# A decayed attention kernel with a feed-forward layer behind it: a second small fetch at the start, and fillers in other places

## The chip, the cores and the metric

The kernel runs on one core of a Trainium2 chip. The metric is the time of one execution on the device, in microseconds (us), as the median of several runs. Of the kernel before, three runs are shown: 191.89, 191.92 and 194.59 us. The core has five engines with instruction streams of their own: TensorE (PE, matmul and its weight loads), VectorE (DVE), ScalarE (ACT), GpSimd (POOL) and SyncE (SP, which here only issues transfers). Sixteen DMA engines move data between the chip's memory (HBM) and the on-chip memory (SBUF). Matmuls write to PSUM.

## The reference

The first half is causal attention with a decay: each of 8 heads has a number lam near 1, and the score of query i and key j counts with lam to the power of i - j. It is computed in blocks of 64 positions, with a state that is carried from block to block.

```python
B, H, S, D = 4, 8, 768, 64
for b in range(S // 64):
    intra = (qb @ kb.T) * Dmask          # Dmask[i, j] = lam ** (i - j) for i >= j, else 0
    out_b = intra @ vb + (qb * lam ** (pos + 1)) @ kv_state
    kv_state = lam ** 64 * kv_state + (kb * lam ** (63 - pos)).T @ vb
```

The second half takes the attention's output as 3072 tokens of 512 numbers through a layer of 2048 hidden numbers:

```python
h = x @ w_in
g = h * sigmoid(1.702 * h)
out = g @ w_out
```

All inputs and the output are float32; q, k and v have the shape [4, 8, 768, 64].

## The kernel before, in words

The sequence is cut into six row tiles of 128 positions (the program's w = 0 to 5), and in each tile all 4 batch entries and all 8 heads are done. The first two tiles (w = 0 and 1) are laid out in another way than the rest: each is done in two halves of the batch (c = 0 and 1), with 256 positions of two batch entries in one tile of 128 partitions. For every tile the kernel loads k, q and v, multiplies k and q by powers of lam while it casts them to bfloat16 (`do_cast`, line 202 or 210), turns them so that the head dimension lies on the partitions, multiplies k by q to scores, masks them (line 271), and multiplies them by v. For w = 0 and 1 the turning is done by TensorE against an identity matrix (`turn_pe`, the matmuls at line 239), and the result is copied out of PSUM by ScalarE (line 222) or VectorE (line 219). For the later tiles a transposing transfer does it (line 246). The feed-forward layer of one tile runs while the next tile's attention is made ready.

What matters here are the first ten microseconds, up to the masks of the first half tile. The order of events in the program is this:

1. ScalarE issues the fetch of `lam_r`, 8 numbers in one partition (line 105). SP issues the loads of k, q and v for w = 0, c = 0, each in two pieces of 256 KB, and then k and q for c = 1 (line 84). ScalarE loads the table for exponentials and logarithms.
2. TensorE runs "fillers": matmuls of a tile of zeros with itself, 512 columns wide, whose result nobody reads (`fill`, line 147). Behind four of them stands the matmul that spreads lam over all 128 partitions (line 151).
3. ScalarE takes the logarithm of lam (line 153) and makes the powers for the casts from it by exponentials (lines 156, 658 and 661), then loads the table for the later activation function (line 663).
4. VectorE casts k in two groups of heads, TensorE turns both, and the same follows for q. Between the turns stand fillers: two behind k's first turn, one behind k's second, one behind q's first, none behind q's second.
5. GpSimd waits at `gate_pool` (line 651) until the second piece of q is there, and only then issues the first load of `w_in` and v for c = 1.
6. The scores (line 260) and the masks on VectorE (line 271) follow.

The order of the work is set in two ways. The part up to the powers (steps 1 to 3) is ordered by the framework's scheduler, which places each instruction on its engine when, by its own reckoning, its inputs are ready. Everything inside `with tc.manual_schedule()` is written out by hand and keeps its order within itself; the scheduler may still take an instruction of that part ahead of one of the first part on the same engine. Each engine then works through its list in order. A transfer carries one of eight semaphores for its completion, handed out in turn, and a new transfer waits until the last one with the same semaphore is done.

SBUF is laid out by pools. The tiles of the pool `const` stand behind one another in the order in which they are made, and the other pools (`ld` for the loads, `work` for casts and turned tiles, `op` for outputs and partial sums) follow behind them.

Of the kernel before, what the change touches and what calls it, by code (L numbers as in the profile page):

```python
# [25 lines left out]
def kernel(  # L26
# [13 lines left out]
    nc = tc.nc  # L40
    f32 = mybir.dt.float32
    bf16 = mybir.dt.bfloat16
    B, H, S, D = q.shape
    P = 128
# [20 lines left out]
    const = ctx.enter_context(tc.tile_pool(name="const", bufs=1))  # L65
# [37 lines left out]

    lam_r = const.tile([1, H], f32)
    nc.scalar.dma_start(out=lam_r, in_=bass.AP(tensor=lam.tensor, offset=lam.offset, ap=[[0, 1], [1, H]]))
    ones = const.tile([1, P], f32)
    nc.vector.memset(ones, 1.0)
    load(0)
# [31 lines left out]
    def acc(name, dt=f32, shape=None, tag="a"):  # L140
        return ps.tile(shape or [P, 4, P], dt, tag=tag, bufs={"a": 5, "mm": 3}[tag], name=name)

    def fill(n, new=None):
        if new:
            fill_ps[0] = acc("ps_fill", shape=[P, W], tag=new)
        for _ in range(n):
            nc.tensor.matmul(fill_ps[0], zero[:, 0:P], zero, start=True, stop=True)  # L147

    fill(4, "mm")
    lam_p = ps.tile([P, H], f32, tag="a", bufs=5, name="lam_p")  # L150
    nc.tensor.matmul(lam_p, ones, lam_r, start=True, stop=True)
    ln_lam = const.tile([P, H], f32)
# [40 lines left out]
    def do_cast(w, c, nm, eng, g=None):  # L193
        if g in (None, 0):
            cast[w, c, nm] = work.tile([P, NP, 2, P] if w < ND else [P, 2, HD], bf16, tag=f"{nm}s{c}",
                                       bufs={"k": 2, "q": 1}[nm], name=f"{nm}s")
        f, x = loaded[w, c, nm], cast[w, c, nm]
        if w < ND:
            pw = {"k": kd_pow, "q": qd_pow}[nm]
            for R in (0, 1) if g is None else (g,):  # L200
                h = slice(4 * R, 4 * R + 4)
                eng.tensor_tensor(x[:, 2 * R : 2 * R + 2].rearrange("p i a (j d) -> p j (i a) d", j=2),
                                  f[:, h].rearrange("p (j i) (a d) -> p j (i a) d", j=2, a=2),
                                  pw[:, h].rearrange("p (j i) a -> p j (i a)", j=2).unsqueeze(3).to_broadcast([P, 2, 4, D]),
                                  op=MUL)
        else:
            pw = {"k": k_pow, "q": q_pow}[nm]
            n = 2 * H // 4
            for j in range(2):
                eng.tensor_tensor(x.rearrange("p b (r i j d) -> p j (b r) i d", i=2, j=2, d=D)[:, j],  # L210
                                  f.rearrange("p h (a d) -> p (h a) d", a=2).rearrange("p (n j i) d -> p j n i d", j=2, i=2)[:, j],
                                  pw.rearrange("p b (r j i) -> p j (b r) i", i=2, j=2)[:, j].unsqueeze(3).to_broadcast([P, n, 2, D]),
                                  op=MUL)
# [19 lines left out]
    def turn_pe(w, c, nm, copy=act_copy, g=None):  # L233
        x = cast[w, c, nm]
        rr = list(range(NP)) if g is None else [2 * g, 2 * g + 1]
        t = acc("ps_t", bf16, [P, len(rr), 2, P])
        for i, r in enumerate(rr):
            for a in range(2):
                nc.tensor.transpose(t[:, i, a, :], x[:, r, a, :], ident)  # L239
        if g in (None, 0):  # L240
            trans[w, c, nm] = work.tile([P, 2 * NP, P], bf16, tag=f"{nm}T{c}", bufs={"k": 1, "q": 2}[nm], name=f"{nm}T")
        copy(trans[w, c, nm][:, 2 * rr[0] : 2 * rr[0] + 2 * len(rr)], t.rearrange("p r a s -> p (r a) s"))
# [407 lines left out]
    def gate_pool(x):  # L650
        nc.gpsimd.tensor_copy(behind_q, x)  # L651
# [4 lines left out]
    with tc.manual_schedule():  # L656
# [4 lines left out]
            nc.scalar.activation(blk_pow[rows].rearrange("p (r i) -> p r i", i=2),  # L661
                                 ln_lam[rows].rearrange("p (r j i) -> p r j i", i=2, j=2)[:, :, j, :], EXP, scale=1.0 * P)
        nc.scalar.activation(warm, q_pow[:, 0, 0:1], GELU)
        fill(3)
        for nm, copies in (("k", (dve_copy, act_copy)), ("q", (act_copy, dve_copy))):
            for g in range(2):
                do_cast(0, 0, nm, nc.vector, g)
            for g in range(2):
                turn_pe(0, 0, nm, copies[g], g)
                fill(2 - g if nm == "k" else 1 - g)  # L670
        gate_pool(loaded[0, 0, "q"][0:1, H // 2, 0:1])
        load_w_in(0)
        load_one(0, 1, "v", v)
# [99 lines left out]
        for i, (c, fc) in enumerate(halves):  # L773
# [8 lines left out]
            if i in (1, 2, 3, 4):  # L782
                nm = "kq"[(i - 1) % 2]
# [37 lines left out]
```

## Time and profile before

| | |
|---|---|
| median of three runs | 191.92 us (191.89 to 194.59) |
| the profiled execution | 192.3 us |
| its span, first to last instruction | 190.6 us |
| TensorE busy | 184.3 us, 97% |
| VectorE busy | 152.0 us, 80% |
| ScalarE busy | 129.8 us, 68% |
| GpSimd busy | 50.7 us, 27% |
| moved by DMA | 33.91 MB, 178 GB/s on average |

The profile is one execution, recorded by the hardware. Its page gives the busy time of each engine, and the chain that ended last: followed back from the last instruction, at each step to what released it. Beside the page the trace can be asked for the timeline of one engine (start, length, line, operation, tiles, and in brackets the idle time before with what ended it), for the transfers in a stretch of time (queue, packets, MB, share of the 16 engines' time) and for the time from issue to landing. "PEld" are TensorE's weight loads, "SPq" and "ACTq" the issuing instructions of SP and ScalarE.

### The profile page before, as it was taken

What the parts mean: (1) busy time and instruction counts of PE and PEld (TensorE: products, weight loads), DVE (VectorE), ACT (ScalarE), POOL (GpSimd) and SP (SyncE); (2) the same over time, 40 slices, a digit from 0 to 9 for tenths busy, and PEclk for the clock granted to TensorE, in tenths of its full rate; (3) what the DMA queues carried; (4) which work ended last, traced back from release to release, by engine and by line L of the source; (5) the groups of instructions that cost most, each with busy time, mean ns of one, the idle gap of its engine ahead of it and who ended that gap; (6) DMA issues with size and microseconds to landing.
All of it is one profiled execution on the core that took longest, in us unless ns stands there. A gap on an engine that the chain in (4) does not pass through costs nothing.

```text
span 190.6 us, 5527 instructions
## 1 busy us (share of the span) xinstructions
PE 184.3 (97%) x2296; PEld 152.2 (80%) x2296; DVE 152.0 (80%) x282; ACT 129.8 (68%) x242; POOL 50.7 (27%) x69
## 2 busy tenths in 40 slices
PE   7998999999999999999999999999999999999993
PEld 2556646887888888888888888888888888888882
DVE  1787599987856799879799879799789797888950
ACT  4957665169776986388895388885488876597611
POOL 5588000063458000294000393000492000000000
PEclk9999999999999999999999999999999999999999
DMA  5999999996997899988998565999555903300113
GB/s 144 317 292 204 205 206 224 310 302 158 215 276 165 193 221 237 215 192 143 213 236 204 183 164 118 212 242 217 184 142 123 209 1 111 112 5 0 55 56 112
DMA packets 89599, 33.91 MB, mean 178 GB/s; under 512 B 67430, under 2 KB 89446, under 8 KB 89574
## 3 DMA queue, kind: packets, MB, share of 16 engines
q1 hardware_dynamic: 84676, 28.84, 60.5%
q0 software_dynamic: 4896, 4.72, 14.4%
q8 instruction: 18, 0.29, 0.7%
q14 instruction: 7, 0.06, 0.1%
q10 hardware_dynamic: 2, 0.00, 0.0%
HBM read 27.26 MB, written 6.29 MB: 176 GB/s over the span
## 4 chain that ended last, share of the span: by engine, by line
PE 92%; DVE 4%; ACT 2%; issue 0%; ACTq 0%; DVEq 0%
PE ps_X L468 22%; PE ps_hX L559 17%; PE ps_V L468 10%; PE ps_hV L559 8%; PE ps_Q L468 6%; PE ps_h L406 5%; PE ps_h L418 5%; PE ps_hQ L559 4%; DVE sm L271 3%; PE ps_t L239 2%; PE ps_s L339 2%; PE ps_o L394 2%; PE ps_fill L147 2%; PE ps_o L381 1%; PE ps_Z L468 1%; PE ps_s L260 1%
## 5 line engine op out<-in xcount | busy, mean ns | idle before, releaser
L468 PEld LDWEIGHTS <-g_s 128*128 128x128 bf16 x384 | 37.0, 98 | 4.9
L578 ACT ACTIVATE g_sb<-h_sb 128x512 bf16<-128x512 f32 x54 | 32.6, 631 | 1.2 <-DVE h_sb L567 1.2
L559 PEld LDWEIGHTS <-w_in_t 128*128 128x128 bf16 x288 | 28.1, 98 | 3.3
L468 PEld LDWEIGHTS <-g_sb 128*128 128x128 bf16 x288 | 27.5, 98 | 4.1
L222 ACT COPY part<-ps_hX 128x512 f32<-128x512 f32 x32 | 18.3, 587 | 11.5 <-PE ps_hX L559 11.5
L468 PE MATMUL ps_X<-w_out_t,g_s 128*128 128x256 bf16 x192 | 23.3, 273 | 0.0
L559 PEld LDWEIGHTS <-w_in 128*128 128x128 bf16 x216 | 21.1, 98 | 2.5
L559 PE MATMUL ps_hX<-x_s,w_in_t 128*128 128x256 bf16 x144 | 21.6, 272 | 0.0
L445 DVE TENSOR_TENSOR g_s<-g_sb 128x1024 bf16<-128x1024 bf16 x24 | 16.3, 687 | 5.8 <-ACT g_sb L578 5.6
L210 POOL TENSOR_TENSOR ks<-kf,k_pow 128x512 bf16<-128x512 f32 x16 | 16.3, 1042 | 4.8 <-DMA kf<-in_k_dram 4.8
L210 POOL TENSOR_TENSOR qs<-qf,q_pow 128x512 bf16<-128x512 f32 x16 | 16.5, 1056 | 3.1 <-DMA qf<-in_q_dram 3.1
L219 DVE COPY part<-ps_hV 128x512 f32<-128x512 f32 x18 | 12.4, 688 | 5.9 <-PE ps_hV L559 5.9
L651 POOL CAST behind_q<-x_s 1x1 f32<-1x1 bf16 x3 | 0.5, 176 | 58.5 <-DVE x_s L544 58.5
L484 ACT COPY part<-ps_X 128x512 f32<-128x512 f32 (+1 forms) x13 | 6.7, 518 | 13.2 <-PE ps_X L468 13.2
L567 DVE TENSOR_TENSOR h_sb<-part,ps_hX 128x512 f32<-128x512 f32 x18 | 12.3, 681 | 2.6 <-PE ps_hX L559 2.1
L567 DVE TENSOR_TENSOR h_sb<-part,ps_hV 128x512 f32<-128x512 f32 x18 | 12.3, 684 | 1.0 <-PE ps_hV L559 1.0
L468 PE MATMUL ps_X<-w_out,g_sb 128*128 128x256 bf16 x96 | 12.6, 273 | 0.0
L468 PE MATMUL ps_Q<-w_out,g_sb 128*128 128x256 bf16 x96 | 12.5, 273 | 0.0
L567 DVE TENSOR_TENSOR h_sb<-part,ps_hQ 128x512 f32<-128x512 f32 x18 | 12.2, 680 | 0.0
L222 ACT CAST v_sb<-vf 128x1024 bf16<-128x1024 f32 (+1 forms) x14 | 12.0, 869 | 0.0
L578 ACT ACTIVATE g_sb<-ps_hX 128x512 bf16<-128x512 f32 x18 | 10.6, 589 | 1.8 <-PE ps_hX L559 1.8
L468 PE MATMUL ps_V<-w_out_t,g_s 128*128 128x256 bf16 x96 | 11.6, 273 | 0.0
(113 smaller groups left out, 354.3 us busy)
## 6 DMA issues: line engine op xcount, KB each, us to landing
kf<-in_k_dram SPq DMA_DIRECT2D x10, 512.0 KB, 6.4
qf<-in_q_dram SPq DMA_DIRECT2D x10, 512.0 KB, 7.2
vf<-in_v_dram SPq DMA_DIRECT2D x10, 512.0 KB, 6.2
out_dram<-o_sb SPq DMA_DIRECT2D x24, 128.0 KB, 2.4
out_dram<-o_sb SPq DMA_DIRECT2D x12, 256.0 KB, 2.8
w_out<-in_moe_w_out_dram POOLq DMA_DIRECT2D x4, 512.0 KB, 14.2
kf<-in_k_dram SPq DMA_DIRECT2D x4, 256.0 KB, 3.1
qf<-in_q_dram SPq DMA_DIRECT2D x4, 256.0 KB, 4.6
```

Of the source, the lines that this page charges most:

```text
L210: eng.tensor_tensor(x.rearrange("p b (r i j d) -> p j (b r) i d", i=2, j=2, d=D)[:, j], f.rearrange("p h (a d) -> p (h a) d", a=2).rearran ...
L219: nc.vector.tensor_copy(out, in_)
L222: nc.scalar.copy(out, in_)
L271: nc.vector.tensor_tensor(sm.rearrange("p i a s -> p i (a s)"), flat, mask_d.rearrange("p o a b s -> p o (a b s)").to_broadcast([P, 2, 2 * ...
L406: nc.tensor.matmul(h, w_in_sb[j][:, kc, i * P : (i + 1) * P], xT[w][:, kc, :], start=(kc == 0), stop=(kc == KC - 1))
L418: nc.tensor.matmul(h[:, u, :], w_in_sb[j][:, kc, i * P : (i + 1) * P], xT[w][:, kc, cols], start=(kc == 0), stop=(kc == KC - 1))
L445: nc.vector.tensor_tensor(o, x, y, op=f)
L468: nc.tensor.matmul(bank[:, t], x[:, m, t * P : (t + 1) * P], y, start=((n in (1, 2, 7) or own) and t == ts[0] * last and m == 0), stop=(m ...
L484: nc.scalar.copy(part[w, n, t.start][:, t], bank[:, t])
L559: nc.tensor.matmul(bank[:, u], z[:, kc], y[:, kc], start=(n in (1, 2, 7) and u + kc == 0), stop=(kc == 1), skip_group_check=True)
L567: nc.vector.tensor_tensor(h, h_part[w, g, {2: 1, 5: 7, 4: 6}[n]], bank, op=ADD)
L578: nc.scalar.activation(g_of[w][:, a : b + 1 : b - a, 256 * i : 256 * i + 256], bank, GELU)
```

## The change

It has three parts. A new tile `first_q`, one number in each of 128 partitions, is fetched behind lam on ScalarE's queue. It takes one number of q for every 3072 (12 KB), over the first quarter of q, which is the first batch entry. Nothing reads the tile. Then the program asks for two fillers ahead of lam's matmul in place of four, and for four in place of three at the start of the hand-ordered part. Last, the fillers between the turns: one behind k's first and two behind k's second (before: two and one), and none behind q's (before: one behind the first).

```diff
     nc.scalar.dma_start(out=lam_r, in_=bass.AP(tensor=lam.tensor, offset=lam.offset, ap=[[0, 1], [1, H]]))
+    first_q = const.tile([P, 1], f32)
+    nc.scalar.dma_start(out=first_q, in_=bass.AP(tensor=q.tensor, offset=q.offset, ap=[[H * S * D // P, P], [1, 1]]))
     ones = const.tile([1, P], f32)
...
-    fill(4, "mm")
+    fill(2, "mm")
     lam_p = ps.tile([P, H], f32, tag="a", bufs=5, name="lam_p")
     nc.tensor.matmul(lam_p, ones, lam_r, start=True, stop=True)
...
-        fill(3)
+        fill(4)
         for nm, copies in (("k", (dve_copy, act_copy)), ("q", (act_copy, dve_copy))):
             for g in range(2):
                 do_cast(0, 0, nm, nc.vector, g)
             for g in range(2):
                 turn_pe(0, 0, nm, copies[g], g)
-                fill(2 - g if nm == "k" else 1 - g)
+                fill(1 + g if nm == "k" else 0)
```

## The prediction

> **What bounds the kernel now.** I read the page first, for the share of each engine; then the chain that ended last over the first 20 us, because every edit lies there; then the timeline of single engines beside it; and last the transfers of the later stages, for what a slower or faster stream would reach.
>
> The page's busy times and its chain:
>
> ```profile
> span 190.6 us, 5527 instructions
> PE 184.3 (97%) x2296; PEld 152.2 (80%) x2296; DVE 152.0 (80%) x282; ACT 129.8 (68%) x242; POOL 50.7 (27%) x69
> PE 92%; DVE 4%; ACT 2%; issue 0%; ACTq 0%; DVEq 0%
> ```
>
> TensorE is the bound: of 190.6 us it is idle for 6.3. A change that leaves the stream of matmuls alone can only win or lose at the edges. This is the edge at the start, as the chain's pieces from 1.39 us on (start, length, work):
>
> ```profile
> 1.39 1.89 PE ps_fill L147 x4
> 3.28 0.54 PE lam_p L151 x2
> ...
> 4.64 0.70 DVE ks L202
> ...
> 5.39 0.61 PE ps_t L239 x4
> 6.00 0.85 PE ps_fill L147 x2
> 6.85 0.43 PE ps_t L239 x4
> 7.28 0.43 PE ps_fill L147
> 7.71 0.44 PE ps_t L239 x4
> ...
> 8.17 0.59 ACT qT L222
> ...
> 8.80 0.47 PE ps_s L260 x16
> ...
> 9.33 2.48 DVE sm L271 x4
> ```
>
> The reader is to see that the start is a single file: four fillers, lam's matmul, its logarithm and powers on ScalarE, the cast of k, then on TensorE k's two turns and q's first turn with three fillers among them, the copy of q, the scores, the masks. From 9.33 VectorE's masks set the pace. So a filler ahead of q's first turn costs its full 0.43 us, and one behind it costs nothing until it touches the masks.
>
> **The change part by part.**
>
> *lam's matmul.* Is it the fillers that hold it, or lam's transfer? The queue of ScalarE's transfers, asked for 1.5 to 1.8 us:
>
> ```profile
> q10 hardware_dynamic: 2, 0.00, 0.3%
> ```
>
> Both packets of lam move in that stretch, so lam is there well before 3.28 and the fillers hold its matmul. Two fillers fewer would be worth having. But the words of the change are not what the built program holds. There the order on TensorE is decided by the framework's scheduler, which pulls fillers out of the hand-ordered part to fill the time that it reckons for lam's transfer. In the changed program four fillers stand ahead of lam's matmul, as before; two follow where three did. So lam's matmul, the powers and k's cast stay where they are: 0 us.
>
> *The fillers behind lam.* The stretch up to k's first turn, on TensorE:
>
> ```profile
> 3.73 1.46 PE L147 MATMUL ps_fill<-zero 128*128 128x512 bf16 x3
> 5.38 0.35 PEld L239 LDWEIGHTS <-ks 128*128 128x128 bf16 x4 [1.10 <-DVE ks L202]
> ```
>
> k's first turn waits for the cast that ends at 5.34, while the third filler's columns end near 5.0. One filler less leaves the turn at 5.39: 0 us. From there the counts are 1, 2, 0 in place of 2, 1, 1 (behind k's first turn, k's second, q's first). Up to q's first turn that is three fillers either way: a turn's matmuls follow each other for 0.43 (the 0.61 of the first has a tail of 0.18 in it), so k's second turn starts at 5.39 + 0.43 + 0.43 = 6.25 (its cast, the second of a pair of 0.70 each from 4.64, is ready by 6.04), the two fillers at 6.68, q's first turn at 7.53, and it is out at 7.53 + 0.61 = 8.14, against 7.71 + 0.44 = 8.15 now. Sum 0. k's second turn is out 0.43 us sooner and q's second about as much, and both meet a closed door:
>
> ```profile
> 7.32 0.59 ACT L222 COPY kT<-ps_t 128x512 bf16<-128x512 bf16 x1
> 6.38 1.28 DVE L202 TENSOR_TENSOR qs<-qf,qd_pow 128x512 bf16<-128x512 f32 x2
> 8.62 0.42 DVE L219 COPY qT<-ps_t 128x512 bf16<-128x512 bf16 x1 [0.96 <-PE ps_t L239]
> ```
>
> ScalarE copies k's second turn at 7.32, when it is through with its own powers and its second table load, and with all of that the change has nothing to do. q's second copy moves from 8.62 to about 8.3, but the masks behind it on VectorE wait for scores that need q's first copy, which stays at 8.17 to 8.76. The masks start at 9.33 as before: 0 us.
>
> *The unread piece of q.* Its issue stands on ScalarE between lam's and the table load:
>
> ```profile
> 0.81 0.51 ACTq L105 DMA_DIRECT2D lam_r<-in_lam_dram  x1
> 1.34 1.28 ACT L110 ACT_TABLE_LOAD   x1 [1.34 <-PEq L805]
> 3.84 0.18 ACT L153 ACTIVATE ln_lam<-lam_p 128x8 f32<-128x8 f32 x1 [1.21 <-PE lam_p L151]
> ```
>
> The row of lam's own issue gives 0.51 us. The table load then ends at 3.13 instead of 2.62, and the logarithm waits until 3.84: hidden, with 0.7 us to spare (if lam were early, this would be the next thing late). Its 128 packets of 4 bytes, 8 on each of the 16 engines, join the stream of k and q. A stretch of 1 us of that stream, first 6 to 7 us, then 4 to 5 us:
>
> ```profile
> q1 hardware_dynamic: 664, 0.33, 109.6%
> q1 hardware_dynamic: 387, 0.19, 79.0%
> ```
>
> A packet takes 1.096 x 16 / 664 = 26 ns in the one and 33 ns in the other, so 8 of them delay the stream by 0.21 to 0.26 us if a tiny packet costs as much as one of 512 bytes, and by nearly nothing if it costs by its bytes; I take 0.2. k is taken up at 4.64, and q's second half here:
>
> ```profile
> 6.98 0.72 POOL L651 COPY behind_q<-qf 1x1 f32<-1x1 f32 x1 [3.59 <-DMA qf<-in_q_dram]
> 5.92 1.86 SPq L84 DMA_DIRECT2D qf<-in_q_dram  x2
> ```
>
> GpSimd waits for q's second half until 6.98 and then issues w_in and v. With 0.2 us of delay the second half's cast ends at 6.38 + 1.28 + 0.2 = 7.86, and q's second turn, which stands at 7.53 + 0.43 = 7.96 now that no filler is before it, is still on time: 0 on the path. The new transfer also takes a place in the round of eight completion semaphores, so that SP's issue of q for the second half of the batch, at 5.92, waits for it instead of for k's first transfer. Issued at about 1.3, ahead of q's own, it lands before q's second half, which is there at 6.98: between nothing and 1 us on a transfer that is first read behind the masks, at 9.33 + 2.48 = 11.81. I take nothing.
>
> *Addresses.* The new tile takes 32 bytes, and in the built program every tile made after it moves by 32. The loads' targets (kf, qf, vf), the stores' source (o_sb) and both sides of the transposing transfers stood at multiples of 256 bytes and now stand 32 beyond one. No row of this case has such a transfer, so I bound it: from nothing to twice as long. What it meets first is the third row tile's q, at the end of which the cover is thinnest:
>
> ```profile
> 47.60 5.01 SPq L88 DMA_DIRECT2D qf<-in_q_dram  x2
> 54.70 2.28 POOL L210 TENSOR_TENSOR qs<-qf,q_pow 128x512 bf16<-128x512 f32 x2 [3.07 <-DMA qf<-in_q_dram]
> 61.66 1.26 SPq L246 DMA_TRANSPOSE qT<-qs  x1
> qT<-qs SPq DMA_TRANSPOSE x2, 2.7
> 65.18 0.62 PE L339 MATMUL ps_s<-qT,kT 64*128 64x128 bf16 x16
> ```
>
> From issue to use q takes 54.70 - 47.60 = 7.1 us, from there GpSimd runs without a gap, and the last transpose lands at 61.66 + 2.7 = 64.36, 0.82 us before the scores. A lengthening up to 0.82 / 7.1 = 12% is hidden. I take the end near nothing, because the nearest rows show the stream not at a fixed rate per packet (26 and 33 ns above), so it is not the write of a packet that sets the pace.
>
> [...]
>
> Sum: 0 on the chain, at most 0.1 from the stream. The profiled execution took 192.3 us (span 190.6); the median of the three runs shown is 191.92, 0.4 lower. Against that median I forecast **192.0 us**.
>
> **The rivals.**
>
> *1. The change does what it says.* lam's matmul starts two fillers, 0.85 us, sooner. The logarithm could then start when the table load ends, 3.13 in place of 3.84: 0.7 us off the whole chain, 191.2. For it: lam is there. Against it: the order in the built program, which the trace of before follows to the instruction. Chance 0.04.
>
> *2. The piece of q opens q's memory ahead of time.* The stretch of 4 to 5 us, where q's transfers begin, moves 387 packets against 664 later. If that is a first touch and the new packets take it over, q lands up to (664 - 387) / 664 = 0.42 us sooner, w_in and v with it. On the chain q waits for TensorE, not for its transfer, so between nothing and all of it would pass, at some later edge: 191.6 at best. Chance 0.11.
>
> *3. TensorE's clock comes later.* The same three fillers as at 3.73, after the turns:
>
> ```profile
> 9.45 0.82 PE L147 MATMUL ps_fill<-zero 128*128 128x512 bf16 x3
> 8.20 0.39 PE L239 MATMUL ps_t<-ident,qs 128*128 128x128 bf16 x4
> ```
>
> They take 0.82 in place of 1.46 us, and the turn at 8.20 is already as short: the clock doubles at about 8 us, though the granted clock reads full throughout. The change leaves TensorE idle for 0.6 us before k's first turn in place of 0.2. If the doubling then comes later, the 16 scores ahead of the masks take 0.94 in place of 0.47, and most of the rest lies beside the masks: +0.5, 192.5, and 0 if it comes before 8.8. Chance 0.14. [...]
>
> *4. The shifted addresses slow the transfers: slower than before.* Place: q's load of the third row tile, then v's load of the next ones. Price: what it lengthens beyond the cover. v's row of the fourth row tile:
>
> ```profile
> 89.41 2.78 SPq L88 DMA_DIRECT2D vf<-in_v_dram  x2
> vf<-in_v_dram SPq DMA_DIRECT2D x2, 512.0 KB, 5.7
> 97.08 1.05 ACT L222 CAST v_sb<-vf 128x1024 bf16<-128x1024 f32 x1
> ```
>
> Its cover is 97.08 - 89.41 - 5.7 = 2.0 us. With 25% longer transfers q costs 1.8 - 0.8 = 1.0 and v nothing: 193. With 45%, 2.4 at q and (2.6 - 2.0) x 3 = 1.8 at v: 4.2, 196.2, and there lies the point from which it is slower by over 2%. Twice as long would be 6.3 and (5.7 - 2.0) x 3 = 11.1, 209. For it: the later stages read tiles whose loads have a cover of 1 to 2 us only. Against it: the packets' times above, which vary with what is read. Chance 0.11, half of it beyond 2%.
>
> **How the numbers follow.** Forecast 0.60 at 192.0, rivals 0.04, 0.11, 0.14 and 0.11. A difference under 2% (3.8 us) is about what a measurement of this kernel can't tell from no change; only rival 4 beyond 45% passes it on the slow side, to which I add 0.005 for what I don't see: 0.06. On the fast side nothing passes it, since the whole start before the masks holds less than 1 us of such waits: 0.01. The range goes from rival 1 at 191.2 to 194.2, which takes in the clock, transfers longer by a third at q (2.3 - 0.8 = 1.5, 193.5), and most of the spread of the three runs shown, which reach 194.59 with nothing changed.
>
> **What would show it.** In the profile after: four fillers and lam's matmul at 3.2 to 3.3; the table load at 1.85; k's first turn at 5.39; q's first turn near 7.5 and no filler between it and the second; the masks at 9.3. Rival 1 shows as lam's matmul near 2.4, rival 2 as more than 387 packets from 4 to 5 us, rival 3 as fillers after the scores that still take 1.4 us, rival 4 as scores of the third row tile later than 65.18 behind a transpose. I am wrong if the masks start more than 0.3 us off 9.33, or if TensorE's idle time beyond 20 us grows.

## The result

The kernel after takes **193.5 us** (median of 22 runs, 192.8 to 194.29). The kernel before, run beside it as often, takes 192.74 us (191.89 to 194.82). The ratio of after to before is **1.0032, with a 95% interval of 1.0016 to 1.0048**: the change makes the kernel about 0.3%, or 0.6 us, slower (the two medians by themselves are 0.76 us apart). That is well under the 2% that count as a difference, but more than the runs leave to chance. The profiled execution took 193.21 us, with a span of 191.4 us.

The page of after: its first lines, the largest transfer queue (packets, MB, share of the time of 16 DMA engines), and the shares of the chain that ended last.

```profile
span 191.4 us, 5524 instructions
...
PE 184.9 (97%) x2294; PEld 152.3 (80%) x2294; DVE 151.3 (79%) x282; ACT 130.0 (68%) x242; POOL 50.4 (26%) x69
...
q1 hardware_dynamic: 84676, 28.84, 69.5%
...
PE 74%; DMA 14%; DVE 3%; POOL 3%; SPq 2%; ACT 1%; issue 1%; POOLq 0%; ACTq 0%
```

The same queue on the page of before:

```profile
q1 hardware_dynamic: 84676, 28.84, 60.5%
```

The busy times of the engines are within 1 us of those of before. Two lines have moved. The same 84676 packets with the same bytes now take 69.5% of the DMA engines' time in place of 60.5%: 0.605 x 16 x 190.6 us / 84676 = 21.8 ns a packet before, 0.695 x 16 x 191.4 / 84676 = 25.1 ns after, 15% more. And the chain that ended last, 92% TensorE before, now goes through transfers for 14% of its length.

First the start, as the timeline of TensorE, ScalarE, VectorE and GpSimd in after (start, length, work, idle time before with what ended it):

```profile
1.39 1.89 PE L149 MATMUL ps_fill<-zero 128*128 128x512 bf16 x4 [1.39 <-DVE zero L119]
3.21 0.59 PE L153 MATMUL lam_p<-lam_r,ones 1*128 1x8 f32 x2
3.73 1.03 PE L149 MATMUL ps_fill<-zero 128*128 128x512 bf16 x2
5.38 0.60 PE L241 MATMUL ps_t<-ident,ks 128*128 128x128 bf16 x4 [0.62 <-DVE ks L204]
...
7.49 1.27 PE L241 MATMUL ps_t<-ident,qs 128*128 128x128 bf16 x8
...
1.35 0.40 ACTq L107 DMA_DIRECT2D first_q<-in_q_dram  x1
1.78 1.28 ACT L112 ACT_TABLE_LOAD   x1 [1.78 <-PEq L807]
3.83 0.18 ACT L155 ACTIVATE ln_lam<-lam_p 128x8 f32<-128x8 f32 x1 [0.77 <-PE lam_p L153]
...
7.40 0.69 DVE L204 TENSOR_TENSOR qs<-qf,qd_pow 128x512 bf16<-128x512 f32 x1 [0.20 <-DMA qf<-in_q_dram]
...
9.55 2.48 DVE L273 TENSOR_TENSOR sm<-ps_s,mask_d 128x512 bf16<-128x512 f32 x4 [0.32 <-PE ps_s L262]
...
7.43 0.70 POOL L653 COPY behind_q<-qf 1x1 f32<-1x1 f32 x1 [4.06 <-DMA qf<-in_q_dram]
```

Four fillers still stand ahead of lam's matmul, and two behind it. k's first turn is where it was, the two turns of q follow each other without a filler, and the masks begin at 9.55 in place of 9.33. The second piece of q lands at 7.43 in place of 6.98, and VectorE's second cast of q waits 0.20 us for it.

Next the stretch from 10 to 46 us, where TensorE loses most of the rest. GpSimd, VectorE, SP and TensorE in before:

```profile
22.04 0.43 DVE L535 TENSOR_TENSOR w_in_t<-w_in 128x512 bf16<-128x512 bf16 x1 [1.67 <-DMA w_in<-in_moe_w_in_dram]
...
38.24 1.29 DVE L202 TENSOR_TENSOR qs<-qf,qd_pow 128x512 bf16<-128x512 f32 x2
40.10 0.69 DVE L482 TENSOR_TENSOR part<-part,ps_X 128x512 f32<-128x512 f32 x1 [0.57 <-PE ps_X L468]
...
29.05 0.77 SPq L654 DMA_DIRECT2D behind<-w_out  x1
...
10.50 3.03 POOL L181 DMA_DIRECT2D w_in<-in_moe_w_in_dram  x4
...
40.71 2.05 POOL L202 TENSOR_TENSOR ks<-kf,kd_pow 128x512 bf16<-128x512 f32 x2 [0.71 <-DMA kf<-in_k_dram]
...
39.83 0.61 PE L239 MATMUL ps_t<-ident,qs 128*128 128x128 bf16 x8
...
43.84 0.62 PE L239 MATMUL ps_t<-ident,ks 128*128 128x128 bf16 x8
```

The same instructions in after:

```profile
23.40 0.43 DVE L537 TENSOR_TENSOR w_in_t<-w_in 128x512 bf16<-128x512 bf16 x1 [2.80 <-DMA w_in<-in_moe_w_in_dram]
...
39.44 1.29 DVE L204 TENSOR_TENSOR qs<-qf,qd_pow 128x512 bf16<-128x512 f32 x2
40.64 0.68 DVE L484 TENSOR_TENSOR part<-part,ps_X 128x512 f32<-128x512 f32 x1
...
30.45 0.77 SPq L656 DMA_DIRECT2D behind<-w_out  x1
...
11.18 3.04 POOL L183 DMA_DIRECT2D w_in<-in_moe_w_in_dram  x4
...
42.86 2.04 POOL L204 TENSOR_TENSOR ks<-kf,kd_pow 128x512 bf16<-128x512 f32 x2 [1.19 <-DMA kf<-in_k_dram]
...
40.25 0.93 PE L241 MATMUL ps_t<-ident,qs 128*128 128x128 bf16 x8
...
44.45 0.91 PE L241 MATMUL ps_t<-ident,ks 128*128 128x128 bf16 x8
...
66.09 0.62 PE L341 MATMUL ps_s<-qT,kT 64*128 64x128 bf16 x16
```

The reader is to see two arms that start at one late transfer. VectorE waits 2.80 us for w_in in place of 1.67, and starts on it at 23.40 in place of 22.04, 1.36 us later. Half of that was there when w_in was issued: GpSimd issues four of its loads from 11.18 on in place of 10.50, because they stand behind its wait for q's second piece (0.45 us later) and behind a cast of k that in after waits 0.24 us for k's transfer. The other half came while w_in was on its way. From 23.40 on VectorE has one short gap (0.35 us for the next piece of w_in, 0.36 in before) until its casts of the second row tile's first half are done: q's cast ends at 39.44 + 1.29 = 40.73 in place of 39.53, and where VectorE had 0.57 us to wait for TensorE at 40.10, it now has none. TensorE's turn of q at 40.25 is stretched from 0.61 to 0.93, because its second half waits for that cast. The other arm goes through SP, whose loads for that row tile stand behind VectorE's work on w_out (the row "behind", 29.05 and 30.45, 1.4 us later). v and k for the second half then come late to GpSimd: k's cast starts at 42.86 in place of 40.71, and ends at 44.9 in place of 42.8. Before, TensorE came to that turn at 43.84, 1.1 us behind the cast; now the turn at 44.45 waits for its second half and takes 0.91 in place of 0.62.

So TensorE is late by 0.22 us at the masks, by about 0.6 behind q's turn, by about 0.85 behind k's, and by 0.91 at the third row tile's scores (66.09 against 65.18). From there it loses nothing more: the two spans differ by 0.8 us.

### The profile page after: what moved, and what is told of

Its sections match the earlier page's. It is cut to its first block, busy times and chain, and to the rows that moved or that the text cites. A ratio compares the mean times of both kernels' runs of the same rounds, so it can differ in the third digit from the quotient of the medians.

```text
span 191.4 us, 5524 instructions
## 1 busy us (share of the span) xinstructions
PE 184.9 (97%) x2294; PEld 152.3 (80%) x2294; DVE 151.3 (79%) x282; ACT 130.0 (68%) x242; POOL 50.4 (26%) x69
## 3 DMA queue, kind: packets, MB, share of 16 engines
q1 hardware_dynamic: 84676, 28.84, 69.5%
## 4 chain that ended last, share of the span: by engine, by line
PE 74%; DMA 14%; DVE 3%; POOL 3%; SPq 2%; ACT 1%; issue 1%; POOLq 0%; ACTq 0%
PE ps_X L470 19%; PE ps_hX L561 16%; PE ps_V L470 9%; PE ps_hV L561 8%; DMA w_in<-in_moe_w_in_dram 6%; PE ps_Q L470 5%; DMA vf<-in_v_dram 4%; PE ps_hQ L561 4%; PE ps_h L420 4%; DMA kf<-in_k_dram 3%; PE ps_s L341 2%; PE ps_o L396 2%; SPq L84 2%; POOL ks L204 2%; DVE w_out_t L434 1%; PE ps_o L383 1%
## 6 DMA issues: line engine op xcount, KB each, us to landing
w_out<-in_moe_w_out_dram POOLq DMA_DIRECT2D x4, 512.0 KB, 14.4
```

## The experiments

Three theories could explain it, and the expectations written down ahead of the runs call them by these letters.

- **A, the addresses.** The new tile moves every tile behind it by 32 bytes, off multiples of 256 bytes, and each transfer to or from them gets slower. In a later set, A1 says that the loads' targets (kf, qf, vf) carry most of it, and its rival that the transposing transfers and the stores do.
- **B, the fetch.** The tiny packets of q (ScalarE's queue moves 146 packets in after and 2 in before) delay the stream at the start.
- **C, the clock.** The fillers in other places leave TensorE idle longer before k's first turn (0.62 us in after, 0.20 in before), and its matmuls get faster later. In before three fillers take 1.46 us at 3.73 and 0.82 at 9.45, with the granted clock at 1.00 in both stretches; that this is a clock was the author's reading.

### The shift alone

The kernel before, with a tile that nothing uses:

```diff
     nc.scalar.dma_start(out=lam_r, in_=bass.AP(tensor=lam.tensor, offset=lam.offset, ap=[[0, 1], [1, H]]))
+    pad = const.tile([P, 1], f32)
     ones = const.tile([1, P], f32)
```

> The kernel before with one unused 32-byte tile where the change has its new one: no fetch, the old fillers, and every later tile 32 bytes further, as in the change. Theory A (the shifted addresses lengthen SP's transfers, and the late loads stall the edge near 45 us): SP's queue takes 69 to 70% of the 16 engines' span in place of 60.5%, q's second piece lands 0.3 to 0.5 us later than 6.98, and the time is 1.002 to 1.004 of before. Theory B (the new fetch's own packets delay the first loads): 60 to 61%, ratio 1.000. Theory C (TensorE's clock comes later because fillers are fewer): ratio 1.000, masks at 9.33.

Measured: 1.0071 (1.0045 to 1.0097) of before, from 6 runs where the other experiments have 12. The queue on its page, and the scores of the third row tile on TensorE behind the first four:

```profile
q1 hardware_dynamic: 84676, 28.84, 68.8%
```

```profile
66.91 0.51 PE L340 MATMUL ps_s<-qT,kT 64*128 64x128 bf16 x12 [0.68 <-DMA qT<-qs]
```

Without any fetch and with the old fillers the queue's share rises as in after, and the kernel is slower, by more than theory A expected. Another part of that expectation failed: q's second piece was there at 7.09, 0.1 us later than before and not 0.3 to 0.5, so the cost isn't bound to that one piece. Here one sees as well the wait that the prediction had named for rival 4: the scores of the third row tile stop for 0.68 us, until q's transposing transfer has landed.

### The change without the shift

The change, with its new tile 256 bytes wide in each partition, of which the fetch still fills 4:

```diff
-    first_q = const.tile([P, 1], f32)
-    nc.scalar.dma_start(out=first_q, in_=bass.AP(tensor=q.tensor, offset=q.offset, ap=[[H * S * D // P, P], [1, 1]]))
+    first_q = const.tile([P, 64], f32)
+    nc.scalar.dma_start(out=first_q[:, 0:1], in_=bass.AP(tensor=q.tensor, offset=q.offset, ap=[[H * S * D // P, P], [1, 1]]))
```

> The whole change, but the new tile is 256 bytes wide (one number of it is fetched, as in the change), so the later tiles stand at multiples of 256 bytes again. Theory A: SP's queue back at 60 to 61%, ratio to before 1.000 to 1.001. Theory B: the first loads stay as late as in the change (q's second piece near 7.4), ratio 1.003. Theory C: masks at 9.5, ratio 1.001 to 1.002.

Measured: 1.0009 (0.9985 to 1.0034). The queue and, on VectorE, w_in and the masks:

```profile
q1 hardware_dynamic: 84676, 28.84, 60.8%
```

```profile
9.55 2.48 DVE L273 TENSOR_TENSOR sm<-ps_s,mask_d 128x512 bf16<-128x512 f32 x4 [0.54 <-PE ps_s L262]
...
22.31 0.42 DVE L537 TENSOR_TENSOR w_in_t<-w_in 128x512 bf16<-128x512 bf16 x1 [1.71 <-DMA w_in<-in_moe_w_in_dram]
```

All three edits of the change are in, only the addresses are as before, and share and wait for w_in (1.71 against 1.67) are those of before. The time alone would not settle it, since its interval reaches to 1.0034. But the shift by itself is slower with nothing else in it, and what it brings, the share and the late w_in, is gone here: the addresses make the slowdown. The masks at 9.55 are here too, and cost nothing that the time shows.

### The fillers alone

The kernel before with the change's three edits of `fill`, and no fetch:

```diff
-    fill(4, "mm")
+    fill(2, "mm")
...
-        fill(3)
+        fill(4)
...
-                fill(2 - g if nm == "k" else 1 - g)
+                fill(1 + g if nm == "k" else 0)
```

> The kernel before with only the fillers of the change (2 asked for ahead of lam, 4 behind, then 1, 2, 0, 0), no new fetch and no new tile. Theory C: the fillers after the scores take 1.0 us or more in place of 0.82, the masks start at 9.5 in place of 9.33, ratio 1.001. Theories A and B: masks at 9.33, ratio 1.000.

Measured: 0.9999 (0.998 to 1.0019). GpSimd's wait for q's second piece, the scores on TensorE and the masks on VectorE:

```profile
7.15 0.70 POOL L651 COPY behind_q<-qf 1x1 f32<-1x1 f32 x1 [3.77 <-DMA qf<-in_q_dram]
...
8.80 0.69 PE L260 MATMUL ps_s<-qT,kT 64*64 64x128 bf16 x32 [0.25 <-ACT qT L222]
...
9.33 0.69 DVE L271 TENSOR_TENSOR sm<-ps_s,mask_d 128x512 bf16<-128x512 f32 x1 [0.31 <-PE ps_s L260]
```

The scores of the run before this one, which has the same fillers:

```profile
8.80 1.07 PE L262 MATMUL ps_s<-qT,kT 64*64 64x128 bf16 x32 [0.25 <-ACT qT L224]
```

The fillers cost nothing, and the masks are at 9.33 as before. The 32 scores start at 8.80 in both runs, behind the same instructions, and take 0.69 us here and 1.07 there: the moment at which the matmuls get faster differs between these two profiles, and the 9.55 of after isn't bound to the fillers. C falls. The run before this one has the fetch and this one has not, so whether chance or the fetch moves that moment is open: with the fetch and lam where it was, the 32 scores take 1.00 to 1.12 us in all four profiles; of the seven without it six are fast (0.69 to 0.72, or two halves of 0.42 each), and one (the rest off, below) takes 1.23. Over the kernels here whose lam is where it was, the masks start anywhere from 9.03 to 9.66, with old and new fillers alike.

### The fetch alone

The kernel before with the fetch, in a tile of 256 bytes as above, and the old fillers:

```diff
     nc.scalar.dma_start(out=lam_r, in_=bass.AP(tensor=lam.tensor, offset=lam.offset, ap=[[0, 1], [1, H]]))
+    first_q = const.tile([P, 64], f32)
+    nc.scalar.dma_start(out=first_q[:, 0:1], in_=bass.AP(tensor=q.tensor, offset=q.offset, ap=[[H * S * D // P, P], [1, 1]]))
```

> The kernel before with only the new fetch, its tile 256 bytes wide so that the later tiles keep their places to the boundary; old fillers. Theory B: q's second piece lands near 7.4 in place of 6.98, ratio 1.002 to 1.003. Theory A and C: q's second piece at most 0.2 us later, ratio 1.000. Rival 2 of the prediction (the fetch opens q's memory): q's second piece earlier than 6.98, ratio 0.998 to 1.000.

Measured: 1.0004 (0.9982 to 1.0025). GpSimd's wait for q's second piece, and the masks on VectorE:

```profile
6.88 0.21 POOL L653 COPY behind_q<-qf 1x1 f32<-1x1 f32 x1 [3.51 <-DMA qf<-in_q_dram]
...
9.61 0.69 DVE L273 TENSOR_TENSOR sm<-ps_s,mask_d 128x512 bf16<-128x512 f32 x1 [0.17 <-PE ps_s L262]
```

q's second piece is there at 6.88, against 6.98 before: no delay by the fetch's packets shows, and they open nothing that shows in the time. B falls. The masks start at 9.61 with the old fillers.

### Which transfers: the loads, or the rest

An unused pool of 32 bytes ahead of the loads' pool and one of 224 behind it, so that kf, qf and vf alone stand 32 bytes off:

```diff
+    pad0 = ctx.enter_context(tc.tile_pool(name="pad0", bufs=1)).tile([P, 8], f32, name="pad0_t")
     ld = ctx.enter_context(tc.tile_pool(name="ld", bufs=2))
+    pad1 = ctx.enter_context(tc.tile_pool(name="pad1", bufs=1)).tile([P, 56], f32, name="pad1_t")
     work = ctx.enter_context(tc.tile_pool(name="work", bufs=2))
```

> The kernel before with two unused tiles of 32 and 224 bytes that put only the targets of the loads (kf, qf, vf) 32 bytes beyond a multiple of 256; everything behind them is back on a multiple. Theory A1 (the loads' writes into SBUF are what the shift lengthens): SP's queue takes 68 to 69% of the span, the loads of 512 KB land as late as with all shifted (k 7.6 to 7.8 us), ratio 1.005 to 1.007. Theory A2 (the reads of the stores and the transposing transfers are lengthened): 61 to 62%, ratio 1.000 to 1.001.

And the other way about, 32 bytes behind the loads' pool, so that all but the loads' targets are off:

```diff
     ld = ctx.enter_context(tc.tile_pool(name="ld", bufs=2))
+    pad1 = ctx.enter_context(tc.tile_pool(name="pad1", bufs=1)).tile([P, 8], f32, name="pad1_t")
     work = ctx.enter_context(tc.tile_pool(name="work", bufs=2))
```

> The other half: kf, qf and vf on multiples of 256 as in the kernel before, and all that lies behind them (the transposing transfers' two sides, the stores' source, and the tiles that only engines use) 32 bytes further. Theory A1: 60.5 to 62%, ratio 1.000. Theory A2: 68 to 69%, ratio 1.005 to 1.007. If engines read shifted tiles slower, busy times of VectorE, ScalarE or TensorE rise in the page with the queue unchanged.

Measured: 1.0011 (0.9992 to 1.0029) with the loads off, 1.0003 (0.9978 to 1.0029) with the rest off. The queue and the median time of q's transposing transfers from issue to landing, with the loads off:

```profile
q1 hardware_dynamic: 84676, 28.84, 66.5%
```

```profile
qT<-qs SPq DMA_TRANSPOSE x8, 2.7
```

With the rest off:

```profile
q1 hardware_dynamic: 84676, 28.84, 61.9%
```

```profile
qT<-qs SPq DMA_TRANSPOSE x8, 3.3
```

The two parts nearly add up: 6.0 of the queue's points come with the loads and 1.4 with the rest, against 8.3 with the shift of everything. The loads carry most of the share, as A1 says, though 66.5% is below its 68 to 69%, and its ratio of 1.005 to 1.007 did not come. The transposing transfers go from 2.7 to 3.3 us when their own tiles are off, and stay at 2.7 when only the loads are. In time neither part alone can be told from nothing, and so how the slowdown divides between them stays open.

### How far a shift matters

The pad of the first experiment, 64 and 128 bytes wide in place of 4 (which take 32):

```diff
-    pad = const.tile([P, 1], f32)
+    pad = const.tile([P, 16], f32)
```

> The kernel before with an unused tile of 64 bytes: all later tiles 64 bytes beyond a multiple of 256. If what counts is whether a piece of 256 or 512 bytes crosses one more boundary of 256 bytes, it costs as much as 32 bytes did: queue 68 to 70%, ratio 1.005 to 1.007. If what counts is a boundary of 64 bytes, nothing: 60 to 61%, ratio 1.000.

```diff
-    pad = const.tile([P, 1], f32)
+    pad = const.tile([P, 32], f32)
```

> The same with 128 bytes. By the boundary of 256 bytes: 68 to 70%, ratio 1.005 to 1.007 again, since each piece still crosses one boundary more. By one of 64 or 128 bytes: 60 to 61%, ratio 1.000. If only the bytes ahead of the boundary cost, less than 32 or 64 bytes or more than them in proportion to the shift.

Measured: 1.0033 (1.0011 to 1.0054) with 64 bytes, 1.0025 (1.0002 to 1.0048) with 128. The queue with 64 bytes:

```profile
q1 hardware_dynamic: 84676, 28.84, 68.7%
```

and with 128:

```profile
q1 hardware_dynamic: 84676, 28.84, 68.2%
```

Any of the three shifts costs the queue the same, 68.2 to 68.8%, and of the widths tried only the multiple of 256 is free of it. The times stay below the 1.005 to 1.007 that was expected. Worked out as above, a packet takes 25.0 ns with the shift of 32 (span 192.2 us), 24.9 with 64 (191.9) and 24.7 with 128 (191.3), against 21.8 in before: about 3 ns more, which don't grow with the shift. Most of that comes with the loads, which write to the shifted tiles (24.0 ns with the loads off, 22.3 with the rest off); what in a transfer takes the time was not shown.

The shift alone cost more in the first experiment (1.0071) than in these two. The intervals overlap at their ends only, the first rests on 6 runs, and no row says why; that stays open.

### lam early, with and without the change

In the built program the scheduler moves fillers of the hand-ordered part ahead of lam's matmul, so that four stand there before and after. An edge that keeps them behind it lets the change do what it says. First in the kernel before, with its old counts between the turns and no fetch:

```diff
-    fill(4, "mm")
+    fill(2, "mm")
...
-    nc.tensor.matmul(lam_p, ones, lam_r, start=True, stop=True)
+    lam_mm = nc.tensor.matmul(lam_p, ones, lam_r, start=True, stop=True)
...
-        fill(3)
+        with tc.issue_after(getattr(lam_mm, "ins", lam_mm)):
+            fill(3)
```

> The kernel before with two fillers ahead of lam's matmul and three behind it, the order held by an edge that keeps the scheduler from taking the three ahead; no fetch, no shift. Rival 1 of the prediction: lam's matmul at 2.4, the logarithm near 3.0, k's cast near 3.8 and the masks near 8.5, ratio 0.996 (191.2 against 191.9). If k's own transfer, there at 3.7 to 4.0, or the clock takes the gain back, the masks stay beyond 9.0 and the ratio is 0.998 to 1.000.

Then in the change with its tile of 256 bytes, where `fill(4)` stands behind that edge:

```diff
-    nc.tensor.matmul(lam_p, ones, lam_r, start=True, stop=True)
+    lam_mm = nc.tensor.matmul(lam_p, ones, lam_r, start=True, stop=True)
...
-        fill(4)
+        with tc.issue_after(getattr(lam_mm, "ins", lam_mm)):
+            fill(4)
```

> The whole change made to do what its words say: the fetch (tile 256 bytes wide, so nothing is shifted), two fillers ahead of lam's matmul and four behind it held in that order, then 1, 2, 0, 0. The logarithm then waits for the table load that the fetch pushes to 3.1, so the masks come 0.7 us before those of the change without shift (9.55 in its profile), ratio 0.997. If lam's place doesn't matter, 1.000 to 1.001 like the change without shift.

Measured: 0.9981 (0.9953 to 1.001) without the fetch, 192.28 us. With it **0.9954 (0.993 to 0.9978)**, 191.84 us, about 0.5% faster than before, while the change as written is slower. TensorE and VectorE without the fetch:

```profile
7.21 0.40 PE L239 MATMUL ps_t<-ident,qs 128*128 128x128 bf16 x4 [0.39 <-DVE qs L202]
...
8.80 1.29 DVE L271 TENSOR_TENSOR sm<-ps_s,mask_d 128x512 bf16<-128x512 f32 x2
```

TensorE, ScalarE and VectorE with it:

```profile
2.35 0.59 PE L153 MATMUL lam_p<-lam_r,ones 1*128 1x8 f32 x2
...
7.02 0.40 PE L241 MATMUL ps_t<-ident,qs 128*128 128x128 bf16 x4 [0.42 <-DVE qs L204]
...
3.08 0.18 ACT L155 ACTIVATE ln_lam<-lam_p 128x8 f32<-128x8 f32 x1
...
8.62 2.49 DVE L273 TENSOR_TENSOR sm<-ps_s,mask_d 128x512 bf16<-128x512 f32 x4
```

lam's matmul starts at 2.35 in place of 3.21. The logarithm then stands behind the table load alone and starts at 3.08 in place of 3.83. q's first turn gains less, 7.02 against 7.49, because it waits for VectorE's cast of q, which starts at 6.28 after 0.58 us of waiting for q's transfer: that is now the next thing late. Without the fetch that turn is at 7.21 and the masks at 8.80. With it the masks start at 8.62, 0.93 us ahead of those of the same change without the edge (9.55). A part of that can be the moment at which the matmuls get faster, which differs from profile to profile (the 32 scores from 8.80 on in 0.69 and in 1.07 us, above). Whether the fetch is worth something once lam is early is not shown: the two kernels' intervals overlap, they differ in the fillers between the turns as well, and VectorE's cast of q starts at 6.28 with the fetch, against 6.46 here without it and 6.10 in the next kernel, also without it.

### The weights' tiles, too

The weights' tiles w_in and w_out stand at no multiple of 256 in any of these kernels. The kernel with lam early and no fetch, with two pads that put them on one and leave all behind them where it was:

```diff
+    pad0 = const.tile([P, 24], f32)
     w_in_sb = [const.tile([P, KC, n * P], bf16, name=f"w_in{j}") for j, n in enumerate(IN_CH)]
...
     w_out_sb = [const.tile([P, CW, d_model], bf16, name=f"w_out{j}") for j in range(NCH)]
+    pad1 = const.tile([P, 40], f32)
```

> As the run with lam's matmul early, and the targets of the two weight loads (w_in, w_out), which stand 160 bytes beyond a multiple of 256 in the kernel before, on multiples as well. If writes that cross a boundary more cost there too, GpSimd's queue takes under 14.4% of the span and w_out lands sooner than 14.2 us; if those loads are bound by their reads (float32 in, half the bytes out), nothing moves against the run without it. Ratio 0.995 to 0.997 if lam's place pays, no less.

Measured: 0.9971 (0.9945 to 0.9997), 192.41 us, against 0.9981 without the pads. The queue of the weights on its page:

```profile
q0 software_dynamic: 4896, 4.72, 14.4%
```

That is the share that this queue has in the kernel without the pads (14.4% as well). These loads, which cast float32 to bfloat16 on their way, show no gain from an aligned target.

### The change once more

The change unaltered, beside the three runs above:

> The change itself, once more, beside the three runs above on one chip. SP's queue 68 to 70%, ratio 1.003 to 1.007, k's cast of the second row tile's second half on GpSimd near 42.8 in place of 40.7.

Measured: 1.003 (1.0009 to 1.0052), 193.44 us. The third row tile's scores on TensorE behind the first four:

```profile
66.38 0.51 PE L341 MATMUL ps_s<-qT,kT 64*128 64x128 bf16 x12 [0.18 <-DMA qT<-qs]
```

The slowdown comes again at its size, with 68.1% in the queue. And the wait at the third row tile's scores, which the first profile of after did not have, shows here with 0.18 us.

### The runs in one table

Ratio to before, share of the queue q1, the start of VectorE's work on w_in, and the start of the masks, each from its own profile:

| | ratio (95% interval) | q1 | w_in | masks |
|---|---|---|---|---|
| before | | 60.5% | 22.04 | 9.33 |
| fillers alone | 0.9999 (0.998 to 1.0019) | 61.1% | 22.75 | 9.33 |
| fetch alone, aligned | 1.0004 (0.9982 to 1.0025) | 60.4% | 22.89 | 9.61 |
| change, aligned | 1.0009 (0.9985 to 1.0034) | 60.8% | 22.31 | 9.55 |
| lam early | 0.9981 (0.9953 to 1.001) | 61.0% | 22.54 | 8.80 |
| lam early, weights aligned | 0.9971 (0.9945 to 0.9997) | 61.0% | 22.74 | 9.00 |
| change, aligned, lam early | 0.9954 (0.993 to 0.9978) | 60.7% | 21.78 | 8.62 |
| the rest off | 1.0003 (0.9978 to 1.0029) | 61.9% | 23.23 | 9.66 |
| the loads off | 1.0011 (0.9992 to 1.0029) | 66.5% | 23.21 | 9.03 |
| shift of 128 | 1.0025 (1.0002 to 1.0048) | 68.2% | 23.30 | 9.32 |
| shift of 64 | 1.0033 (1.0011 to 1.0054) | 68.7% | 23.42 | 9.65 |
| shift of 32 | 1.0071 (1.0045 to 1.0097) | 68.8% | 23.45 | 9.14 |
| the change | 1.0032 (1.0016 to 1.0048) | 69.5% | 23.40 | 9.55 |
| the change once more | 1.003 (1.0009 to 1.0052) | 68.1% | 23.36 | 9.55 |

The reader is to see that ratio and masks don't go together, while w_in splits the kernels in two: 21.78 to 22.89 where loads, transposes and stores are aligned, 23.21 to 23.45 where something is off. The first range is 1.1 us wide with aligned addresses alone, and before's 22.04 stands early in it, so that a part of the 1.36 us in after can be the spread of single executions. And a late w_in isn't enough by itself: with the loads off or the rest off it is as late as with a shift of 128 (23.21, 23.23 and 23.30), and the time can't be told from that of before.

## Why the prediction was right, and where it was not

192.0 us was forecast, within 191.2 to 194.2, and a difference under 2% with a chance of 0.93. 193.5 us lies in the range and the change is under 2%. Of the 1.5 us between, 0.8 is the kernel before itself, whose median over 22 runs is 192.74 and not 191.92; the rest is the slowdown, where the sum had 0 to 0.1. So the number lies in the range because the range had room for a slower stream and for the spread of the runs. The sum did not have the 0.6 us; they came by rival 4, which had a chance of 0.11. Of the two signs named for being wrong, the masks stayed inside theirs (0.22 us off). The other showed, though faintly: TensorE's idle time beyond 20 us grew from 3.5 to 3.7 us in after, and to 4.3 with the shift alone, where the change without the shift has 3.4.

- **lam's matmul: right.** Four fillers, lam at 3.21 (forecast 3.2 to 3.3), and the powers and k's cast where they were. That the words of the change were not what the built program held decided this step. The edge that makes the words true gives 0.9954, 0.9 us; rival 1 had priced it at 0.7.
- **The fillers behind lam: right.** k's first turn at 5.38 (5.39), q's first at 7.49 (7.53), the time alone 0.9999. The masks started at 9.55, inside the 0.3 that was granted around 9.33.
- **The issue on ScalarE: right.** It took 0.40 us (0.51 taken from lam's row), the table load ended at 1.78 + 1.28 = 3.06 (3.13), and the logarithm still waited 0.77 us for TensorE.
- **The packets of the fetch: mis-sized, without effect.** 0.2 us of delay was taken for q's second piece, from a bound at which a packet of 4 bytes costs as much as one of 512. It came 0.45 later (7.43; 7.17 when the change ran once more), but 0.1 sooner (6.88) where the fetch is there and the addresses are aligned. So the packets show no cost, the lower bound. What made it 0.45 in that one execution isn't told apart: with the fillers alone, where neither packets nor addresses differ from before, the piece landed at 7.15 in place of 6.98.
- **The new transfer's completion semaphore: right.** Nothing was taken for it. SP's issue of q for the second half of the batch starts at 5.87 and 6.10 with the fetch and aligned addresses, against 5.92 in before, 6.36 with the fillers alone and 6.39 in after.
- **Addresses: the step that failed.** Its words were "I take the end near nothing, because the nearest rows show the stream not at a fixed rate per packet (26 and 33 ns above), so it is not the write of a packet that sets the pace." Measured over the whole kernel, the time of a packet rises from 21.8 to 25.1 ns, 15%. That is not near nothing. The 0.1 that the sum allows from the stream is a term that no run shows; in its place the runs showed these 15% and 0.6 us in the time. The inference was wrong: that packets' times vary between two stretches says that something else adds to them, not that the write adds nothing. That a tile's address can cost was seen, but its price was argued from a row that doesn't bear on it. An estimate: with 15%, q's 7.1 us would grow by 1.1, and about 0.25 would pass the cover of 0.82: less than half of the 0.6 measured, so the places were short as well as the price.
- **The cover: one of three places.** The prediction held that the third row tile's q is met first, with 12% of cover, and v after it. That place is real: the scores waited for q's transposing transfer by 0.68 us with the shift alone and by 0.18 in the second profile of the change. But 0.7 of the 0.9 us in the first profile of after came earlier, between 10 and 46 us, where w_in delays VectorE's casts and SP's loads of the second row tile. The prediction followed the later row tiles' transfers, whose own addresses move. w_in's target was off a multiple of 256 before and after: it is late because GpSimd issues it behind q's and k's transfers (0.68 of 1.36 us), and the rest comes while it shares the DMA engines with them. How much of each is the spread of single executions isn't told apart.
- **Rival 4, the addresses, 0.11:** this is what happened, for the most part at an earlier place than it named, and with packets 15% longer, between its end at nothing and its 25%. The 45% at which it would have passed 2% was far off.
- **Rival 2, q's memory opened ahead, 0.11:** its mark is there, though not only with the fetch, and its gain is not. From 4 to 5 us the queue moved 554 packets in after, 544 with the fetch alone, and 387 and 315 in before and with the fillers alone, which looks as if the fetch brought the stream into its stride sooner. But with the rest off, without any fetch, it moved 538, so that isn't shown. q's second piece was there 0.1 us sooner, of the 0.42, no more than it varies without the fetch (6.98 and 7.15), and the time gained nothing (1.0004).
- **Rival 3, a later clock, 0.14:** that three fillers take 0.82 us in place of 1.46 is in the rows of before, that a clock doubles is not: the granted clock reads 1.00 from 3 to 7 and from 7 to 10 us, in before and in after. A delay of this kind is in the profile of after, 0.22 us at the masks, but it is there with the old fillers too (9.61 with the fetch alone, 9.66 with the rest off), it is not there with the fillers alone (9.33), and those cost nothing.

The queue rows of that stretch from 4 to 5 us, in after:

```profile
q1 hardware_dynamic: 554, 0.27, 106.3%
```

and with the fillers alone:

```profile
q1 hardware_dynamic: 315, 0.16, 52.9%
```

## What to carry to other kernels

A new tile can cost more than its bytes: look where it puts the tiles behind it, and give a small one that stands ahead of the targets of transfers a width of 256 bytes in each partition. Here that took the ratio from 1.0032 to 1.0009. Compare the share of a queue at equal packets and bytes, before the time: it showed some 8 points in a single execution, where the time needed a dozen runs or more for a third of a per cent. And when transfers get slower, follow all that share the engines with them, not only those whose own tiles moved, and the engine that issues them: it may itself be waiting for one of the slower ones.

## What was not expected of the hardware

A shift by 32, 64 or 128 bytes brings the queue to the same share, 68.2 to 68.8% in place of 60.5%, so for these it is the multiple of 256 that counts and not the distance from it. Loads from float32 to bfloat16 on GpSimd's queue showed none of it (14.4% with their targets on and off it). And the moment at which TensorE's matmuls get faster differs between executions whose TensorE work is the same up to there (32 scores in 0.69 or in 1.07 us from 8.80 on), though the granted clock is 0.998 and 1.0 over these two executions, and reads 1.00 from 7 to 10 us in before, where the scores take 0.71, as in after, where they take 1.12. What makes the moment differ is not shown, and the fetch, which the two kernels with the longer scores have, isn't excluded as a part of it.
